# A low-rank mixer behind gated attention: down of the last batch's six chunks as two threes

## The chip, the cores and the metric

The kernel runs on one core of a Trainium2 chip. The core has a matrix engine (PE, with its weight loads shown apart as PEld), a vector engine (DVE), a scalar engine (ACT), a general engine (POOL) and a queue engine (SP) that only issues DMAs and handles semaphores. The engines run side by side and wait for one another by semaphores; each takes its own instructions strictly in order. The metric is the time of one execution on the device in microseconds (us).

## The reference

The inputs are `q`, `k`, `v`, `a_re`, `a_im` of shape (4, 8, 768, 48): four batches, eight heads, 768 steps, 48 numbers. The first half is a gated linear attention with a complex gate, the second a token mixer of low rank and a channel mixer. All is in float32.

```python
mag = sqrt(a_re**2 + a_im**2); scale = minimum(mag, 0.999) / (mag + 1e-6)
a_re_n, a_im_n = a_re * scale, a_im * scale
for t in range(S):                       # S_re, S_im: (B, H, 48, 48), zero at first
    new_re = ar * S_re - ai * S_im
    new_im = ar * S_im + ai * S_re
    S_re, S_im = new_re + outer(k[t], v[t]), new_im
    y[:, :, t] = q[t] @ S_re
x = y, heads side by side                # (4, 768, 384)
h = transpose(transpose(x) @ U @ V)      # U: (768, 32), V: (32, 768)
u = x + h
out = u + maximum(u @ w_ch1, 0) @ w_ch2  # w_ch1: (384, 1536), w_ch2: (1536, 384)
```

## The kernel before

**Tiling.** The 4 x 768 steps are cut in 24 chunks of 128 (`CH`). The attention takes one chunk after another: `prep(i)` (L847) weighs q and k, turns them on PE and keeps them in a tile `QK` of three in a ring; `chain(i)` (L881) computes the chunk's own products and the running state; the gates come from `gates(g)` (L649) for two chunks at a time. Each batch has six chunks, and its mixing starts when all six are there, since the product with U and V runs over all steps. `mixer(m)` (L974), m = 0 to 11, takes two chunks: `spread` and `mixed` make u in the tiles `xo` (one row of 384 for each step, L1016), `turned` transposes it to `uT`, then "up" is the product with `w_ch1` (`w1` in the code) and the maximum with 0, giving `h` (12 tiles of 128 channels by 256 steps), and "down" the product with `w_ch2` (`w2`), which is added to `xo`; `leave` stores the result. The last batch is m = 9, 10, 11, chunks 18 to 23.

**Fewer products.** From m = 2 on, up is done for two chunks at once as a product of a 3 by 3 by a 3 by 2 arrangement of blocks (`up_fewer`, L1110): 15 block products of 4 matmuls where the plain way has 18. Their right sides are sums of u's blocks (L1133), their left sides w1's blocks or sums of them, made once (L1214). They run as five chains A to E; in a chain PSUM accumulates, and after each step the chain's running total is added to one of the six outputs, so that a step's effect on the others cancels by the choice of the sums. From m = 1 on, down is done by `down_two` (L1253) as a 2 by 2 by 2 arrangement: 7 block products of 6 matmuls (128 by 128 times 128 by 192; `product` with its matmul in L1293) where the plain way has 8. For it the vector engine makes eight sums of h of 384 columns (L1285) and adds six totals of 192 and one of 384 to xo (`onto`, by L463). The sums of w2 that it needs stand in the tile `stage` (`W2S`), those of h in `stage` and `more` (`HS`).

**Order.** Every operation is added to a plan with an engine, a cost and what it reads and writes; but the sequence in which they are emitted is a list of numbers in the file, `ORDER` (L31), one common order for all engines. Each engine's instructions stand in that order. `Plan.order` (L151) checks that nothing comes before what it needs and that a ring's buffer is not taken too early. The costs do not decide anything when `ORDER` is there. DMA issues are in the same order: loads on SP, in-between moves and most stores on POOL; the stores of m = 11 on SP (L1237).

**The check at the end.** The quick form of the attention is valid only if the gates are in range. `judge` (L1418) reduces tables of minima and maxima, among them `least`, to one number: three pairs of small matmuls (L1433 to L1435, the group named "bad ps" in the plan) and a cast to `flag` (L1437). Behind the list of operations every engine loads that number into a register and branches on it:

```python
found = nc.values_load(flag, min_val=0, max_val=512, ...)   # L1468
with tc.If(found != 0, preferred_fallthrough_block=False):  # L1478
    in_general(...)                                          # the general, slow way
```

With the inputs at hand the number is 0, and the general way is not entered. L1523 carries the program's closing instructions.

## Time and profile before

The median of three executions is 536.64 us (536.31 to 537.48). The profiled execution took 537.17 us, with a span of 535.4 us from its first instruction to its last.

| | busy us | share of the span | instructions |
|---|---|---|---|
| PE (matmuls) | 515.6 | 96% | 7506 |
| PEld (weight loads) | 469.7 | 88% | 7506 |
| DVE | 419.7 | 78% | 837 |
| ACT | 295.3 | 55% | 528 |
| POOL | 32.2 | 6% | 61 |

DMA moved 39.95 MB, 75 GB/s on the mean; the granted clock of the matrix engine was 0.998 of full speed.

How to read the rows that follow in the prediction. A row of the 40 slices has one digit for each fortieth of the span, the busy share in tenths. A row of a group names line, engine, operation, result and sources, shapes (partitions by elements) and how often; behind the bar stand busy time, mean ns of one, and the idle time of the engine just ahead with what ended it. A row of the timeline starts with the start and the length in us. In the chain that ended last each row is a start, a length and the work that the end hung on. An engine's name with a q is its sequencer: loads of registers, branches, semaphores.

### The profile page before, as it was taken

The page shows a single profiled execution, that of the slowest core. Times are in us where ns is not written, and L with a number is a line of the kernel's source. Part 1 is how long each engine was busy: PE and PEld are TensorE (multiplying, and loading weights), DVE is VectorE, ACT ScalarE, POOL GpSimd, SP SyncE. Part 2 cuts the span into 40 slices and gives each one's busy share as a digit, 9 for nine tenths or more (in the row PEclk, how much of TensorE's full clock was granted, in tenths as well). Part 3 has the DMA queues.
Part 4 walks back from the last instruction along what each step waited for, and adds up shares of the span by engine and source line. Part 5 has one row for each costly group of instructions (what it writes and reads, how often), then busy time and mean ns, then how long its engine had stood idle before and what let it go on. Part 6 is the DMA issues. An engine that isn't in the chain of part 4 may idle for free.

```text
span 535.4 us, 17159 instructions
## 1 busy us (share of the span) xinstructions
PE 515.6 (96%) x7506; PEld 469.7 (88%) x7506; DVE 419.7 (78%) x837; ACT 295.3 (55%) x528; POOL 32.2 (6%) x61
## 2 busy tenths in 40 slices
PE   2899999999999999999999999999999999999995
PEld 1787786857989998999999999999999999999995
DVE  7898988999999997997887877797786735745543
ACT  5889998893776866546647847256345212020100
POOL 1000000001020001001100101100110000000010
PEclk9999999999999999999999999999999999999999
DMA  9967886565233424502524334200250000000011
GB/s 227 191 122 198 181 143 171 165 114 109 43 73 94 61 48 84 106 1 40 116 44 89 55 62 90 48 1 1 42 105 24 4 1 1 1 2 31 22 38 36
DMA packets 150690, 39.95 MB, mean 75 GB/s; under 512 B 145912, under 2 KB 147408, under 8 KB 150608
## 3 DMA queue, kind: packets, MB, share of 16 engines
q1 hardware_dynamic: 148400, 34.43, 32.3%
q0 software_dynamic: 2208, 4.35, 2.4%
q8 instruction: 61, 1.00, 0.8%
q14 instruction: 21, 0.17, 0.1%
HBM read 33.60 MB, written 4.76 MB: 72 GB/s over the span
## 4 chain that ended last, share of the span: by engine, by line
PE 82%; DVE 9%; ACT 4%; DMA 2%; issue 1%; SPq 1%; DVEq 0%; ACTq 0%
PE down L1293 29%; PE few L1161 13%; PE bank L1161 12%; PE bank L870 4%; PE bank L899 4%; PE bank L957 4%; PE bank L919 3%; PE bank L949 2%; PE up L1054 2%; PE bank L1016 1%; PE bank L745 1%; PE bank L809 1%; DVE QKC L460 1%; DMA stage<-in_moe_w_ch_dram 1%; ACT QK L876 1%
## 5 line engine op out<-in xcount | busy, mean ns | idle before, releaser
L1293 PE MATMUL down<-w,h 128*128 128x192 f32 x396 | 72.7, 330 | 0.0
L1293 PEld LDWEIGHTS down<-w,h 128*128 128x128 f32 x396 | 64.6, 190 | 1.0
L876 ACT COPY QK<-bank 112x512 f32<-112x512 f32 x96 | 51.3, 592 | 17.2 <-PE bank L870 17.0
L463 DVE TENSOR_TENSOR xo<-down,xo 128x192 f32<-128x192 f32 (+1 forms) x79 | 29.9, 385 | 30.9 <-PE down L1293 30.8
L457 ACT ACTIVATE gate<-gate 128x768 f32<-128x768 f32 (+1 forms) x50 | 39.7, 796 | 17.3 <-DVE wide L717 13.7
L460 DVE TENSOR_TENSOR QKC<-qk,cs 128x768 f32<-128x768 f32 x48 | 44.9, 952 | 3.7 <-ACT cs L457 3.6
L1169 ACT COPY h<-bank 128x512 f32<-128x512 f32 x25 | 14.6, 586 | 57.8 <-PE bank L1161 57.8
L1293 PE MATMUL down<-stage 128*128 128x192 f32 x198 | 37.9, 330 | 0.0
L1054 PE MATMUL up<-uT,w 128*128 128x256 f32 x144 | 34.0, 385 | 0.2
L1293 PEld LDWEIGHTS down<-stage 128*128 128x128 f32 x198 | 32.3, 190 | 0.8
L454 ACT ACT_TABLE_LOAD x24 | 30.8, 1283 | 1.1 <-PEq L1512 0.7
L1054 PEld LDWEIGHTS up<-uT,w 128*128 128x128 f32 x144 | 26.6, 190 | 5.0 <-DVE xo L463 0.5
L1237 POOL DMA_DIRECT2D out_dram<-xo x32 | 19.1, 625 | 193.6 <-DVE xo L463 104.8
L1169 ACT COPY h<-few 128x512 f32<-128x512 f32 x35 | 20.3, 586 | 18.5 <-PE few L1161 18.0
L870 PE MATMUL bank<-ident,QKC 64*112 64x64 f32 x768 | 29.1, 221 | 1.0 <-DVE G L466 0.4
L457 ACT ACTIVATE es<-bank 128x384 f32<-128x384 f32 x48 | 20.3, 495 | 17.6 <-PE bank L745 16.5
L1161 PE MATMUL bank<-extra,w 128*128 128x128 f32 x232 | 29.9, 275 | 0.0
L870 PEld LDWEIGHTS bank<-ident,QKC 64*112 64x112 f32 x768 | 24.3, 130 | 6.3 <-issue 1.6
L795 POOL DMA_DIRECT2D gate<-F x15 | 12.5, 834 | 284.8 <-DVE F L818 166.5
L969 ACT COPY xo<-bank 64x192 f32<-64x192 f32 x48 | 14.7, 314 | 24.6 <-PE bank L949 23.9
L1161 PEld LDWEIGHTS bank<-extra,w 128*128 128x128 f32 x232 | 28.1, 192 | 0.1
L457 ACT ACTIVATE cs<-F 128x384 f32<-128x384 f32 x48 | 23.7, 518 | 6.8 <-DVE F L818 6.6
(187 smaller groups left out, 1179.1 us busy)
## 6 DMA issues: line engine op xcount, KB each, us to landing
stage<-in_moe_w_ch_dram SPq DMA_DIRECT2D x12, 768.0 KB
gate<-in_a_re_dram SPq DMA_DIRECT2D x24, 192.0 KB
gate<-in_a_im_dram SPq DMA_DIRECT2D x24, 192.0 KB
qk<-in_q_dram SPq DMA_DIRECT2D x24, 192.0 KB
qk<-in_k_dram SPq DMA_DIRECT2D x24, 192.0 KB
VP<-in_v_dram SPq DMA_DIRECT2D x24, 192.0 KB
out_dram<-xo POOLq DMA_DIRECT2D x12, 192.0 KB, 2.4
out_dram<-xo POOLq DMA_DIRECT2D x20, 96.0 KB, 2.4
```

The source lines that it names most:

```text
L454: ACT(1.4, rank, lambda: nc.scalar.preload_act_table_set(name), writes=[TABLE])
L457: return nc.scalar.activation(out=o, in_=i, func=f, **kw)
L460: nc.vector.tensor_tensor(out=o, in0=a, in1=b, op=OP.mult)
L463: nc.vector.tensor_tensor(out=o, in0=a, in1=b, op=OP.add)
L870: nc.tensor.transpose(out=get(*ps[r])[0:DQ, h], in_=get(*qkc)[at, h].rearrange("p u d -> p (u d)")[:, 0:DQ], identity=ident[at, at], tile_ ...
L876: nc.scalar.copy(out=get(*QK)[:, u].rearrange("p (h t) -> p h t", t=CH)[:, :, r * HC:(r + 1) * HC], in_=get(*ps[r])[0:DQ])
L899: nc.tensor.matmul(out=get(*ps0)[r:r + HC, h], lhsT=k_of(h, r, HC), rhs=q_of(h, r, HC), start=True, stop=True, tile_position=(0, r))
L957: nc.tensor.matmul(out=get(*y[u])[side(r, u), p], lhsT=q_of(h, r * HC, HC), rhs=get(*(mid_G if r else ("G", i - 1)))[:, h], start=(p == 0) ...
L1054: nc.tensor.matmul(out=get(*ps)[:, e], lhsT=w1[:, f, (ff + e) * 128:(ff + e + 1) * 128], rhs=get(*uT)[:, f], start=(f == 0), stop=(f == KD ...
L1161: nc.tensor.matmul(out=get(*ps)[:, q], lhsT=w()[:, q * 128:(q + 1) * 128], rhs=v[0](), start=(n == 0 and q == 0), stop=True, skip_group_ch ...
L1169: ACT(c_act(n3 * CH) - 0.045, RU, lambda i=i, k=k: nc.scalar.copy(out=at(i, k), in_=get(*ps)), [ps], [o])
L1293: nc.tensor.matmul(out=get(*to)[:, part], lhsT=x(j), rhs=y[:, j], start=(first and j == 0), stop=(j == KH - 1), skip_group_check=not first)
```

## The change

- The constant `THREE` = 9. Mixers 1 to 8 keep `down_two`. Mixers 9, 10 and 11 no longer have a down of their own.
- In its place `down_three(t)`, t = 0 and 1, takes three chunks at once (18 to 20, 21 to 23) as a 3 by 3 by a 3 by 2 arrangement: three chunks, three thirds of the 1536 channels (4 tiles of 128), two halves of the 384 outputs. There are 15 block products of 4 matmuls of the same tile, in chains A to E as in `up_fewer`. For each t there are 13 sums of h's blocks of 512 columns and 15 additions of a total of 192 columns to `xo`.
- `prepare()`, called in mixer 9, makes w2's sums on the vector engine (3 of 384 columns, 12 of 768) and three copies of 384 columns on ACT. They stand in buffers that the attention has left (`qk`, `es`, `cs`, `QKC`, planes of the gate tile, `GL`) and one in `stage`.
- The h of mixers 10 and 11 stands in three buffers `hq` from the ring of `QK`, whose tiles get 128 partitions in place of `DQ` for it. The sums of h stand in `stage` for t = 0 and in `w1` for t = 1.
- Stores: chunks 18 to 20 go whole, on POOL; 21 and 23 whole and 22 in two halves, on SP.
- `ORDER` is changed. PE's order is the same up to its place 409 of 647, the end of mixer 5's down; behind that attention of chunks 18 to 23, mixers 6 to 8 and the last batch interleave anew: up of 9, 10 and 11, with the first three's products among the last of these, and then the second three. The six matmuls of `judge` are the last of PE and the cast to `flag` the last of DVE. Before that, on DVE, the copy of uT for mixer 1 stands behind two more steps, and the reductions into `least` of the groups 8 to 10 stand earlier, as does, on SP, the reload of the tables T that they read.

In the diff the lists of numbers in `ORDER` are left out but for the ones at the early and the last places.

```diff
@@ ORDER @@
...
-    608, 607, 605, 614, 726, 701, 64, 615, 441, 616, 251, 61, 442, 443, 444, 445, 255, 420, 56, 421, 256, 422, 423, 446, 60, 448, 59, 405, 447, 424,
-    406, 617, 618, 619, 620, 453, 494, 407, 57, 62, 704, 632, 257, 621, 63, 408, 495, 67, 496, 680, 634, 497, 414, 409, 70, 631, 454, 622, 635, 636,
+    608, 607, 605, 614, 726, 701, 64, 615, 441, 616, 251, 61, 442, 443, 444, 445, 255, 420, 56, 421, 256, 422, 423, 446, 60, 448, 59, 405, 424, 406,
+    617, 618, 447, 619, 620, 453, 494, 407, 57, 62, 704, 632, 257, 621, 63, 408, 495, 67, 496, 680, 634, 497, 414, 409, 70, 631, 454, 622, 635, 636,
...
-    2174, 2175, 2176, 2179, 2180, 2181, 2102, 2019, 2023, 2097,
+    2181, 2179, 2201, 2093, 2182, 2188, 2099, 2180, 2184, 2191, 1691, 2189, 2185, 2190, 2194, 2186, 2192, 2195, 2187, 2203, 2204, 2094, 2193, 2196,
+    2102,
@@ -344,6 +345,7 @@
     DH = DM // 2
     PLAIN = 1
+    THREE = 9
     FEWER, SINGLE, AHEAD = 2, 3, 1
     NCH = S // CH
     NT = B * NCH
@@ -848,7 +850,7 @@
-        buffer(QK, "QK", 3, [DQ, 2, H * CH])
+        buffer(QK, "QK", 3, [128, 2, H * CH])
...
@@ -998,12 +1000,30 @@
         uT, h = ("uT", m), ("h", m)
+        k3 = KF // 3
+        def third(n, j):
+            return ("h", n) if n == THREE else ("hq", ((n - THREE - 1) * 3 + j) // 2)
+        def third_of(n, j, k):
+            return third(n, j) + ((j, k),)
+        def third_at(n, j, k):
+            a = get(*third(n, j))
+            a = a[:, j * k3:(j + 1) * k3] if n == THREE else a[:, ((n - THREE - 1) * 3 + j) % 2].rearrange("p (f t) -> p f t", t=N)
+            return a[:, :, k * CH:(k + 1) * CH]
         if ahead or m >= AHEAD:
             buffer(uT, "uT", 2, [128, KD, N])
             if ahead:
                 ring(h, "hx", [extra.rearrange("p (f t) -> p f t", t=N)])
-            else:
+            elif m <= THREE:
                 buffer(h, "h", 1, [128, KF, N])
+            elif m == THREE + 1:
+                for n in range(KF // k3):
+                    buffer(("hq", n), "QK", 3, [128, 2, H * CH])
@@ -1148,7 +1168,7 @@
             put(1, lambda: x(11), lambda: b(2, 0), lambda: b(2, 1), OP.subtract, (), (11,))
             def at(i, k):
-                return get(*h)[:, n3 * i:n3 * (i + 1), k * CH:(k + 1) * CH]
+                return get(*h)[:, n3 * i:n3 * (i + 1), k * CH:(k + 1) * CH] if m < THREE else third_at(m, i, k)
             seen, left = set(), {}
             def chain(tag, steps):
@@ -1160,8 +1180,8 @@
                         for q in range(n3):
                             nc.tensor.matmul(out=get(*ps)[:, q], lhsT=w()[:, q * 128:(q + 1) * 128], rhs=v[0](), start=(n == 0 and q == 0),
                                              stop=True, skip_group_check=True)
-                    PE(0.893, RM, products, [uT, ("w1", 0, 0)] + [c_of(k) for k in range(8)] + [x_of(k) for k in v[1]], [ps], takes=[h],
-                       steps=2 * n3)
+                    PE(0.893, RM, products, [uT, ("w1", 0, 0)] + [c_of(k) for k in range(8)] + [x_of(k) for k in v[1]], [ps],
+                       takes=[h if m < THREE else third(m, to[0])], steps=2 * n3)
                     i, k = to
                     o = ("part", (m, i, k))
                     if to not in seen:
@@ -1172,7 +1192,7 @@
                     else:
                         DVE(c_dve(n3 * CH), RU, lambda i=i, k=k: nc.vector._custom_dve(
                             dve_ops.TENSOR_ADD_SAT, out=at(i, k), in0=get(*ps), in1=at(i, k), s0=math.inf, s1=0.0), [ps, o],
-                            [h + (n3 * i,), h + (n3 * i + 2,)])
+                            [h + (n3 * i,), h + (n3 * i + 2,)] if m < THREE else [third_of(m, i, k)])
                     left[to] = left.get(to, total_of[to]) - 1
                     yield
@@ -1332,6 +1352,161 @@
             product(two, 0, lambda j: of_s(2, j), w2_of(1, 1), lambda half: [("s2", 0, half)], first=False)
             onto(ua, 1, two, 0)
             leave(0, 1)
+        def w2_third(j, y, x=None):
+            a = w2[:, j * k3:(j + 1) * k3, y * DH:(y + 1) * DH]
+            return a if x is None else a.rearrange("p (j x) m -> p j x m", x=2)[:, :, x]
+        def w2_names(j):
+            return [("w2", f) for f in range(j * k3, (j + 1) * k3, 2)] + [("w2i", 0)]
+        def flat_of(n):
...
+        def second(j):
+            return lambda: flat_of(12 + j)
+        def prepare():
+            places = [("qk", None)] * 2 + [("es", None)] * 2 + [("cs", None)] * 2 + [("qkc", QKC)] * 3 + [
+                ("gx", AREA["x"]), ("gy", AREA["y"]), ("gar1", AREA["ar"][0:1])]
...
+            RW, W = ("w2x", 0), k3 * DH
+            for j in range(3):
+                DVE(c_dve(W // 2), RW, lambda j=j: nc.vector.tensor_tensor(
+                    out=flat_of(12 + j)[:, 0:k3:2], in0=w2_third(j, 1, 1), in1=w2_third(j, 1, 0), op=OP.subtract), w2_names(j), [("w2x", 12 + j, 0)])
+                ACT(c_act(W // 2), RW, lambda j=j: nc.scalar.copy(out=flat_of(12 + j)[:, 1:k3:2], in_=w2_third(j, 1, 1)), w2_names(j),
+                    [("w2x", 12 + j, 1)])
+            def b(j, k):
+                return (lambda: w2_third(j, 0), w2_names(j)) if k == 0 else (second(j), [("w2x", 12 + j)])
+            def x(n):
+                return (lambda: flat_of(n)), [("w2x", n)]
+            def put(n, p, q, op):
+                DVE(c_dve(W), RW, lambda: nc.vector.tensor_tensor(out=flat_of(n), in0=p[0](), in1=q[0](), op=op), p[1] + q[1],
+                    [("w2x", n)] + [("w2s", 0), ("s1", 0), ("s2", 0)] * (n == 11))
+            sub_, add_ = OP.subtract, OP.add
+            put(3, b(0, 0), b(1, 0), sub_)
+            put(4, x(3), b(2, 0), add_)
+            put(10, b(0, 0), b(2, 0), add_)
+            put(5, x(4), b(1, 1), add_)
+            put(8, b(0, 1), b(2, 1), add_)
+            put(6, b(2, 1), x(4), sub_)
+            put(1, b(0, 1), b(1, 1), sub_)
+            put(7, b(0, 0), b(2, 1), add_)
+            put(0, b(0, 0), b(1, 1), sub_)
+            put(2, b(1, 0), b(1, 1), sub_)
+            put(11, b(2, 0), b(2, 1), sub_)
+            put(9, b(0, 1), b(0, 0), sub_)
+        def down_three(t):
+            i1, RS = (B - 1) * NCH + 3 * t, ("three", t)
+            def a(i, j):
+                n, k = divmod(i1 + i, MC)
+                return (lambda: third_at(n, j, k)), [third_of(n, j, k)]
+            kept = [("hc", (t, n)) for n in range(8)]
+            def c_at(n):
+                if n in (0, 3):
+                    return a(0, 2)[0]() if n == 0 else a(2, 1)[0]()
+                z = {1: 0, 2: 1, 4: 2, 5: 3, 6: 4, 7: 5}[n]
+                place = w1[:, z // 3] if t else parts[z // 3]
+                return place[:, z % 3 * k3 * CH:(z % 3 + 1) * k3 * CH].rearrange("p (f t) -> p f t", t=CH)
+            def c_of3(n):
+                return a(0, 2)[1] if n == 0 else a(2, 1)[1] if n == 3 else [kept[n]]
+            def c(n):
+                return (lambda: c_at(n)), c_of3(n)
+            def put(n, p, q, op):
+                DVE(c_dve(k3 * CH), RS, lambda: nc.vector.tensor_tensor(out=c_at(n), in0=p[0](), in1=q[0](), op=op), p[1] + q[1],
+                    c_of3(n) + ([] if n in (0, 3) else [("w1", 0), ("w1", 1)] if t else [("w2s", 0), ("s1", 0), ("s2", 0)]))
+            sub_, add_ = OP.subtract, OP.add
+            put(6, a(2, 0), a(2, 1), add_)
+            put(4, c(6), a(0, 1), sub_)
+            put(5, c(6), a(1, 1), sub_)
+            put(6, a(1, 1), a(2, 1), sub_)
+            put(6, c(6), a(2, 2), sub_)
+            put(7, a(0, 2), a(0, 0), sub_)
+            put(2, a(1, 2), c(7), sub_)
+            put(1, c(7), a(2, 2), sub_)
+            put(7, a(0, 1), a(0, 2), add_)
+            put(7, c(7), a(1, 2), sub_)
+            put(3, a(1, 0), c(2), sub_)
+            put(3, c(3), c(5), sub_)
+            put(0, a(2, 2), a(0, 1), sub_)
+            def u(j, k):
+                return (lambda: w2_third(j, 0), w2_names(j)) if k == 0 else (second(j), [("w2x", 12 + j)])
+            def v(n):
+                return (lambda: flat_of(n)), [("w2x", n)]
+            total_of, seen = {(0, 0): 2, (0, 1): 3, (1, 0): 3, (1, 1): 2, (2, 0): 2, (2, 1): 3}, {}
+            def out_at(i, lo, hi):
+                n = i1 + i
+                b, cc = where(n)
+                def f(queue):
+                    queue.dma_start(out=out[b, cc * CH:(cc + 1) * CH, lo:hi], in_=get("xo", n)[:, lo:hi])
+                o = ("xo", n) if hi - lo == DM else ("xo", n, lo // DH)
+                if t:
+                    SP(0.6, ("load", 0), lambda: f(nc.sync), [o], [("out", n)])
+                else:
+                    POOL(0.55, R0, lambda: f(nc.gpsimd), [o], [("out", n)], late=0.6)
+            def run(tag, steps):
+                ps = ("down", (THREE + t, tag))
+                psum(ps, "Y", [128, DH], [128, 512])
+                for n, (w, x, to) in enumerate(steps):
+                    def products(n=n, w=w, x=x):
+                        for q in range(k3):
+                            nc.tensor.matmul(out=get(*ps), lhsT=w[0]()[:, q], rhs=x[0]()[:, q], start=(n == 0 and q == 0), stop=(q == k3 - 1),
+                                             skip_group_check=True)
+                    PE(1.3, ("mixing", THREE + t), products, w[1] + x[1], [ps], steps=2 * k3)
+                    i, k = to
+                    o = ("xo", i1 + i)
+                    def onto(o=o, k=k):
+                        z = get(*o)[:, k * DH:(k + 1) * DH]
+                        add(z, get(*ps), z)
+                    DVE(c_dve(DH), R0, onto, [ps], [o + (k,)])
+                    seen[to] = seen.get(to, 0) + 1
+                    if seen[to] == total_of[to]:
+                        if t and i == 1:
+                            out_at(i, k * DH, (k + 1) * DH)
+                        elif seen.get((i, 1 - k), 0) == total_of[(i, 1 - k)]:
+                            out_at(i, 0, DM)
+                    yield
+            A = run("A", [(c(0), v(4), (2, 0)), (a(2, 2), v(6), (2, 1)), (c(1), u(2, 1), (0, 1)), (c(2), v(7), (0, 0)),
+                          (c(3), u(0, 0), (1, 0)), (a(1, 0), v(9), (1, 1))])
+            Bc = run("B", [(a(0, 1), v(5), (0, 1)), (c(4), u(1, 1), (2, 1)), (c(5), v(0), (1, 1)), (a(1, 1), v(2), (1, 0)),
+                           (c(6), v(3), (2, 0))])
+            Cc = run("C", [(a(1, 2), v(11), (1, 0)), (c(7), v(10), (0, 0))])
+            D3 = run("D", [(a(0, 0), v(8), (0, 1))])
+            E = run("E", [(a(2, 0), v(1), (2, 1))])
+            for g in (A, Bc, D3, A, Bc, E, A, Bc, Cc, A, Bc, Cc, A, Bc, A):
+                next(g)
         if ahead:
             turned()
@@ -1361,7 +1536,12 @@
         if m == PLAIN:
             DVE(c_dve(KH * DH), R0, lambda: nc.vector.tensor_tensor(out=w2_of(0, 1), in0=w2_of(1, 1), in1=w2_of(0, 1),
                                                                     op=OP.subtract), [("w2s", 0)], ALL_W2 + [("w2i", 0)])
-        down_two()
+        if m < THREE:
+            down_two()
+        if m == THREE:
+            prepare()
+        elif m > THREE:
+            down_three(m - THREE - 1)
```

More of the change, by code (lines that the diff above doesn't have):

```diff
@@ new lines, in second @@
+        def second(j):
[3 more added lines that the diff above has]
+                ("gx", AREA["x"]), ("gy", AREA["y"]), ("gar1", AREA["ar"][0:1])]
+            shapes = {"qk": [128, 2, H, D], "es": [128, 2, DM], "cs": [128, H, 2, D]}
+            order = [12, 13, 3, 4, 10, 0, 1, 2, 5, 6, 7, 8, 14, 9]
+            for n, (tag, tiles) in zip(order, [("GL", GL), ("gai1", AREA["ai"][0:1])] + places):
+                if tiles is None:
+                    buffer(("w2x", n), tag, 2, shapes[tag])
+                else:
+                    ring(("w2x", n), tag, tiles)
+            RW, W = ("w2x", 0), k3 * DH
[24 more added lines that the diff above has]
+            put(9, b(0, 1), b(0, 0), sub_)
```

15 lines of the change are left out of this document (12 added, 3 removed), and 70 rows, old and new, of the table ORDER.

## The prediction

> **What bounds the kernel now.** I read the page first (totals and the 40 slices), then the busy time by stretches for the part that the change rewrites, then the timeline and the queue rows of the last microseconds, since those settle what follows the last matmul.
>
> ```profile
> span 535.4 us, 17159 instructions
> PE 515.6 (96%) x7506; PEld 469.7 (88%) x7506; DVE 419.7 (78%) x837; ACT 295.3 (55%) x528; POOL 32.2 (6%) x61
> PE   2899999999999999999999999999999999999995
> 516.32 13.67 PE down L1293 x84
> ```
>
> ```profile
> 330.00:430.00 100.00, 100.00 (x1691) 96.69 (x1690) 75.87 (x156) 45.52 (x90) 6.90 (x11) 1.00 0.17 35
> 430.00:460.00 30.00, 30.00 (x302) 28.70 (x301) 15.65 (x40) 4.80 (x10) 0.00 (x0) 1.00 0.01 2
> 460.00:490.00 30.00, 30.00 (x243) 29.46 (x242) 18.03 (x44) 4.00 (x7) 1.61 (x3) 1.00 0.04 14
> 490.00:515.00 25.00, 25.00 (x191) 24.71 (x190) 11.44 (x28) 3.52 (x6) 1.72 (x4) 1.00 0.04 13
> 515.00:536.00 21.00, 14.98 (x99) 14.61 (x98) 8.38 (x19) 0.00 (x0) 1.50 (x3) 0.93 0.14 46
> ```
>
> In a row of the second fence stand the bounds, the length, then the busy time of PE, PEld, DVE, ACT and POOL, the granted clock and the DMA share. PE is without a gap from 330 us to its last matmul at about 530 us, at clock 1.00, while DVE is half idle after 430 us. So from 330 us on the time is the number of matmuls times their pitch, plus what stands behind the last matmul. The whole kernel from 10% in is nearly so too; only the first slices are not.
>
> Behind the last matmul there are 5.4 us, and they need rows of their own:
>
> ```profile
> 514.94 0.19 PE L1433 MATMUL bank<-ones,bad 128*1 128x1 f32 x2
> 520.26 0.36 DVE L463 TENSOR_TENSOR xo<-down,xo 128x192 f32<-128x192 f32 x1 [1.21 <-PE down L1293]
> 520.53 0.14 DVE L1437 CAST flag<-bank 1x1 int32<-1x1 f32 x1
> ...
> 526.89 1.14 PE L1293 MATMUL down<-w,stage 128*128 128x192 f32 x6
> 527.86 1.14 PE L1293 MATMUL down<-w,h 128*128 128x192 f32 x6
> 528.84 1.14 PE L1293 MATMUL down<-w,more 128*128 128x192 f32 x6
> 529.04 0.56 DVE L463 TENSOR_TENSOR xo<-down,xo 128x384 f32<-128x384 f32 x1 [1.63 <-PE down L1293]
> 530.01 0.36 DVE L463 TENSOR_TENSOR xo<-down,xo 128x192 f32<-128x192 f32 x1 [0.42 <-PE down L1293]
> ```
>
> ```profile
> L1468 ACTq TENSOR_LOAD <-flag x1: 460/460/460, 520.7 to 520.7; - x1
> L1468 POOLq TENSOR_LOAD <-flag x1: 496/496/496, 520.7 to 520.7; - x1
> L1468 PEldq TENSOR_LOAD <-flag x1: 487/487/487, 527.5 to 527.5; - x1
> ```
>
> ```profile
> L1478 PEldq COMPARE_BRANCH  x2: 90/2116/4141, 528.1 to 530.3; - x2
> L1478 POOLq INC_SWDGE_SEM  x1: 1123/1123/1123, 521.8 to 521.8; - x1
> ```
>
> ```profile
> L1523 POOLq DRAIN  x3: 46/112/3975, 525.5 to 535.1; - x3
> L1523 SPq DRAIN  x3: 7/7/7, 534.2 to 534.8; - x3
> L1523 PEldq DRAIN  x2: 8/38/68, 534.5 to 534.9; - x2
> ```
>
> A queue row gives min/median/max in ns, then the first and the last start. The kernel sums up its range checks in one number (matmuls of L1433 to L1435, cast L1437); every engine loads it (L1468) and branches on it (L1478) to a fallback that is not entered. Today this is over early: cast at 520.53, POOL loads at 520.7, and its closing run (load, semaphore reset of 1.12, branches, a drain of 3.98 that starts at 525.5) ends at 529.4, hidden under the last ten microseconds of matmuls. It can only be the first of the three drains that took 3975 ns, as the others lie within the last 0.9 us. POOL then waits for PE, whose second branch (530.3, 4.14 long) and drain (534.5) are what the end at 535.4 hangs on.
>
> **Matmuls: fewer by six.** Mixers 9, 10, 11 did 7 products of 6 matmuls each, 3 x 42 = 126; the threes do 2 x 15 products of 4, 120. Matmul tile and stream stay 128x128 by 192. The PE rows above start 0.975 us apart for three matmuls (six records), 0.325 us each: 6 x 0.325 = **-1.95 us**, all on the bounding engine.
>
> **Vector work: about +20 us, on an engine that has room.** These rows price it:
>
> ```profile
> L460 DVE TENSOR_TENSOR QKC<-qk,cs 128x768 f32<-128x768 f32 x48 | 44.9, 952 | 3.7 <-ACT cs L457 3.6
> L463 DVE TENSOR_TENSOR xo<-down,xo 128x192 f32<-128x192 f32 x66 | 22.8, 353 | 28.3 <-PE down L1293 28.2
> L1285 DVE TENSOR_TENSOR h<-h 128x384 f32<-128x384 f32 x22 | 12.1, 551 | 0.0
> L463 DVE TENSOR_TENSOR xo<-down,xo 128x384 f32<-128x384 f32 x13 | 7.2, 552 | 2.6 <-PE down L1293 2.6
> L1214 DVE TENSOR_TENSOR extra<-extra,w 128x512 f32<-128x512 f32 x4 | 2.7, 684 | 0.0
> ```
>
> Added: w2's sums, 12 of 768 elements (12 x 0.952) and 3 of 384 (3 x 0.551); the sums of h, 26 of 512 (26 x 0.684); 30 adds of 192 (30 x 0.353): 11.4 + 1.7 + 17.8 + 10.6 = 41.5 us. Removed: 24 sums of 384 (13.2), 18 adds of 192 (6.4), 3 of 384 (1.7): 21.2. Net +20.3. From 430 us on DVE is idle for 106 - 53.5 = 52.5 us by the four stretch rows, and idle 24.1 of the 100 before that. ACT's three new copies of 384 lie in an engine that is busy under 5 us in 30. So I cost them at nothing as work; the cover is PE's unbroken run. What may cost is where they stand: a product of a three needs a whole sum first, and a total is added to xo before its PSUM tile's next step may run on, with five tiles in turn. Bounds: 0, since the order puts products of another mixer or another chain between two steps of one chain, and +2.0, about two waits as long as the 0.975 pitch of a product. Below nothing is excluded here, as PE has no gap from 330 us that could be filled. I take **+0.5**, near the lower end, since the old closing, with seven products through two tiles, shows no PE gap.
>
> **Moved in the common order.** Up to PE's place 409 of its order (some 329.5 us) no PE instruction moves. On DVE the copy of uT for mixer 1 moves behind two other steps:
>
> ```profile
> 90.02 0.56 DVE L1040 COPY uT<-bank 128x384 f32<-128x384 f32 x1 [0.89 <-PE bank L1035]
> ```
>
> It sat idle 0.89 us waiting here, and steps that were ready now go first. That gains up to 0.89 where DVE is the limit and nothing where PE is; the neighbouring slices of PE are full, so I take **-0.2** (bounds -0.9 and 0).
>
> The reductions 'least 8' to 'least 10' of the gate tables go earlier on DVE, the last from some 350 to about 330 us, and with it on SP's queue the reload of table T10 right behind the store of TD.
>
> ```profile
> 325.29 0.43 SPq L760 DMA_DIRECT2D TD<-es  x1
> SPq L763 <- DMA TD<-es: 4.9, 3, 2.2
> ```
>
> SP then waits for TD to land; the longest such wait was 2.2 us. Queued behind it are only input loads of chunks used much later. Store 325.3, landing 2.2 and the reload of the same order put T10 at about 330, when DVE comes to it; at most 1 us of DVE, which costs PE nothing at once. It is inside the +0.5 and its bounds. Outputs of chunks 18 to 20 go whole on POOL (48 issues become 45), the last three on SP (one more issue, of the kind of 0.4 to 0.6 us): 480 KB late in place of 288. They land while the engines close, so 0.
>
> **The closing: the check goes last.** In the changed order the matmuls of the check are the last instruction of PE and the cast is the last of DVE, behind the last add; before, both were some ten microseconds ahead. Nothing needs the number earlier; but every engine's load of it now waits for the end. Call T the end of the last product's matmuls. The last add now starts 0.03 after it (530.01 against 529.98), the cast 0.27 behind the add's start (520.53 against 520.26), the load 0.17 behind the cast: loads at T + 0.47. PE's own way from there is load 0.49, first branch 0.1 to 0.2, second branch 4.14, drain 0.07, some 0.3 between: T + 5.7. POOL's is its run of 520.7 to 529.4 (525.5 + 3.98), 8.7 us: **T + 9.2**. After the slowest engine comes the closing barrier, 0.9 us (PE's drain of 534.5 ends at 534.5, the span at 535.4). End at T + 10.1, where it was T + 5.4 (535.4 - 529.98): **+4.7 us** (4.66 unrounded). Bounds: by PE alone T + 6.6, +1.2 (POOL's drain free); above, +4.66 with 0.9 more if POOL's writes, which then end nearer, lengthen its drain.
>
> [...]
>
> **Sum.** -1.95 + 0.5 - 0.2 + 4.66 = +3.0. The profiled run of before took 537.17 (span 535.4 and 1.8 around it), 0.5 above the median 536.64 of the three; against the median: **539.6 us**, 0.56% slower. Its own range runs from 536.64 - 1.95 - 0.9 + 4.66 = 538.5 to 536.64 - 1.95 + 2.0 + 4.66 + 0.9 = 542.3. What a measurement tells from no change is about 0.2%, 1.07 us.
>
> **Rivals.**
> Rival 1: POOL's 3.98 us drain is not owed behind the check; it stood waiting for something that ends in any case (its last outputs, say), and would be short at the end. Then PE's branch sets the end, +1.2: -1.95 + 0.5 - 0.2 + 1.2 = -0.45, **536.2**. For it: the other two drains of POOL took 46 and 112 ns. Against it: the last of its outputs was issued by 516.5, 9 us before that drain, and such a write lands in 2.4 us (last figure of the second row).
>
> ```profile
> 514.36 2.14 POOL L1237 DMA_DIRECT2D out_dram<-xo  x4 [15.60 <-DVE xo L463]
> ```
>
> ```profile
> out_dram<-xo POOLq DMA_DIRECT2D x12, 192.0 KB, 2.4
> ```
>
>  [...]
>
> Rival 2, faster: the closing runs of both PE and POOL are waiting for something outside that starts at the last output, and the load's place costs nothing. Then -1.65: **535.0**. It decides if POOL needs less than 4.1 us from load to drain's end (T + 0.47 + 4.1 + 0.87 = T + 5.4) and PE too. Against it: POOL's run of before ended at 529.4, ahead of the last output.
>
> Rival 3: the new order stalls PE from 330 us on, by the 20 us of DVE or by T10; three or four waits of a product's pitch more than I took, +2 to +3.4: **541.6 to 543**. For it: the order puts the 30 products between other work, and whether their sums are ready there no row of before shows. Against: 52 us of idle DVE.
>
> **Chances.** My forecast 0.70, rival 1 0.13, rival 2 0.07, rival 3 0.10. The time is that of the first. The range 536.0 to 541.5 leaves out rival 2, rival 3 and the tip of the forecast's own, 0.2 in all. Faster by over 0.2%: rival 2 and 0.02 of rival 1 (its uT gain at the full 0.9); within 0.2%: the rest of rival 1; slower: forecast and rival 3.
>
> **What would show it.** The cast of the flag is the last DVE row, and all five loads of the flag start together at about 528.5 to 529. PE full from 330 us to a last matmul near 528.3, with 120 products' matmuls on the threes' line. POOL's semaphore reset, branch and a drain of about 4 us behind the loads, ending at 537 to 538 as the last before the closing barrier. If POOL's drain there is a fraction of a microsecond, rival 1 holds; if PE shows waits on DVE after 330 us that sum to over 2 us, rival 3. The prediction is wrong if PE's end comes later than 530, or the span's end less than 8 us behind it.

## The result, and the profile after

The changed kernel takes 541.01 us in the median (540.88 to 541.96, four executions) where the kernel before took 537.06 beside it: a ratio of 1.0078, 95% interval 1.0058 to 1.0097. It is slower, as forecast, by 3.95 us in place of 3.0. The profiled execution took 540.94 with a span of 539.1.

From the page of the changed kernel (span, totals, PE's row of the 40 slices), and its busy time by stretches (bounds, length, PE, PEld, DVE, ACT, POOL, clock, DMA share):

```profile
span 539.1 us, 17163 instructions
PE 514.8 (95%) x7494; PEld 468.9 (87%) x7494; DVE 438.3 (81%) x863; ACT 295.6 (55%) x531; POOL 30.5 (6%) x58
PE   2899999999999999999999999999999999999992
```

```profile
330.00:430.00 100.00, 99.92 (x1674) 96.59 (x1673) 78.27 (x150) 44.99 (x91) 6.85 (x11) 1.00 0.17 35
430.00:460.00 30.00, 30.00 (x301) 28.74 (x300) 18.72 (x48) 5.02 (x11) 1.08 (x2) 1.00 0.03 11
460.00:490.00 30.00, 30.00 (x268) 29.42 (x268) 24.72 (x52) 6.84 (x13) 0.00 (x0) 1.00 0.01 1
490.00:515.00 25.00, 25.00 (x164) 24.83 (x163) 19.50 (x42) 0.47 (x1) 1.07 (x2) 1.00 0.04 12
515.00:540.00 25.00, 14.00 (x91) 13.67 (x89) 5.42 (x18) 0.00 (x0) 1.07 (x2) 0.86 0.12 42
```

PE is nearly as full as before, and DVE is busier by the 19 us that were added; PE's last slice has a digit of 2 where it had 5. What changed most is the end. From the timeline of the changed kernel:

```profile
522.12 1.46 PE L1484 MATMUL bank<-stage,hq 128*128 128x192 f32 x8
523.42 1.46 PE L1484 MATMUL bank<-w,hq 128*128 128x192 f32 x8
...
527.32 1.46 PE L1484 MATMUL bank<-gate,hq 128*128 128x192 f32 x8
528.71 0.19 PE L1613 MATMUL bank<-ones,bad 128*1 128x1 f32 x2
...
528.82 0.36 DVE L465 TENSOR_TENSOR xo<-bank,xo 128x192 f32<-128x192 f32 x1 [0.68 <-PE bank L1484]
529.10 0.13 DVE L1617 CAST flag<-bank 1x1 int32<-1x1 f32 x1
```

And its queue rows behind that (min/median/max in ns, first and last start):

```profile
L1648 ACTq TENSOR_LOAD <-flag x1: 586/586/586, 529.3 to 529.3; - x1
L1648 POOLq TENSOR_LOAD <-flag x1: 612/612/612, 529.3 to 529.3; - x1
...
L1658 PEldq COMPARE_BRANCH  x2: 90/1946/3803, 530.0 to 530.3; - x2
L1658 POOLq INC_SWDGE_SEM  x1: 1063/1063/1063, 530.5 to 530.5; - x1
...
L1703 POOLq DRAIN  x3: 46/112/3728, 534.6 to 538.9; - x3
```

The last product ends at T = 527.32 + 1.46 = 528.78, 1.20 ahead of the kernel before (529.98). The loads of the flag start together at 529.3, T + 0.5 (SP's at 529.6). PE is through its long branch at 534.1. POOL's drain starts at 534.6 and ends at 538.28, and 0.86 us behind that the span ends: T + 10.36, where it was T + 5.39 (spans of 539.14 and 535.37, to two decimals). So the matmul part gained 1.20 us and the closing lost 4.97: +3.77 of span.

### The profile page after: what moved, and what is told of

It is laid out like the page before. It is cut to its first block, busy times and chain, and to the rows that moved or that the text cites. A ratio compares the mean times of both kernels' runs of the same rounds, so it can differ in the third digit from the quotient of the medians.

```text
span 539.1 us, 17163 instructions
## 1 busy us (share of the span) xinstructions
PE 514.8 (95%) x7494; PEld 468.9 (87%) x7494; DVE 438.3 (81%) x863; ACT 295.6 (55%) x531; POOL 30.5 (6%) x58
## 4 chain that ended last, share of the span: by engine, by line
PE 85%; DVE 9%; ACT 2%; issue 1%; DMA 1%; SPq 0%; DVEq 0%; ACTq 0%
PE down L1313 21%; PE few L1181 13%; PE bank L1181 12%; PE bank L1484 7%; PE bank L872 4%; PE bank L901 4%; PE bank L959 4%; PE up L1074 3%; PE bank L921 3%; PE bank L951 2%; PE bank L1036 1%; PE bank L747 1%; PE bank L811 1%; PE bank L751 1%; DVE QKC L462 1%
## 5 line engine op out<-in xcount | busy, mean ns | idle before, releaser
L878 ACT COPY QK<-bank 112x512 f32<-112x512 f32 x96 | 51.3, 591 | 20.3 <-PE bank L872 20.1
L1313 PE MATMUL down<-w,h 128*128 128x192 f32 x288 | 53.5, 331 | 0.0
L1313 PEld LDWEIGHTS down<-w,h 128*128 128x128 f32 x288 | 47.0, 190 | 0.8
L465 DVE TENSOR_TENSOR xo<-bank,xo 128x192 f32<-128x192 f32 x78 | 25.7, 351 | 16.7 <-PE bank L1484 12.2
L465 DVE TENSOR_TENSOR xo<-down,xo 128x192 f32<-128x192 f32 (+1 forms) x58 | 22.0, 387 | 11.8 <-PE down L1313 11.6
L459 ACT ACTIVATE es<-bank 128x384 f32<-128x384 f32 x48 | 20.3, 496 | 16.7 <-PE bank L747 15.6
L1313 PE MATMUL down<-stage 128*128 128x192 f32 x144 | 27.7, 331 | 0.0
L901 PE MATMUL bank<-QK 112*64 112x64 f32 x768 | 26.7, 224 | 0.0
L901 PEld LDWEIGHTS bank<-QK 112*64 112x64 f32 x768 | 24.2, 138 | 1.4 <-issue 0.2
```

Of the source, the lines that this page charges most:

```text
L459: return nc.scalar.activation(out=o, in_=i, func=f, **kw)
L465: nc.vector.tensor_tensor(out=o, in0=a, in1=b, op=OP.add)
L878: nc.scalar.copy(out=get(*QK)[0:DQ, u].rearrange("p (h t) -> p h t", t=CH)[:, :, r * HC:(r + 1) * HC], in_=get(*ps[r])[0:DQ])
L901: nc.tensor.matmul(out=get(*ps0)[r:r + HC, h], lhsT=k_of(h, r, HC), rhs=q_of(h, r, HC), start=True, stop=True, tile_position=(0, r))
L1313: nc.tensor.matmul(out=get(*to)[:, part], lhsT=x(j), rhs=y[:, j], start=(first and j == 0), stop=(j == KH - 1), skip_group_check=not first)
```

## The experiments

Times are compared with executions of the kernel before that were taken beside them. T is again the end of the last product.

**The check early again.** The check's steps are moved back ahead of the end (in this run the cast stands at 515.2, 14 us ahead of T); its PSUM tile comes from the ring that is free by then.

```diff
-        psum(ps, "T", [128, 1], [128, 512])      # in judge
+        psum(ps, "M", [128, 1], [128, 512])
 ORDER (numbers of the changed kernel):
-    2181, 2179, 2201, 2093, ... 2195, 2187, 2203, 2204, 2094, 2193, 2196, 2102,
+    2156, 2200, 2202, 2201, 2088, ... 2095, 2203, 2169, ... 2170, 2204, 2159, ... 2187, 2094, 2193, 2196, 2102,
```

> The changed kernel with one thing undone: the check's last steps (edges, three pairs of small matmuls, cast) stand some 17 us ahead of the end again; for this the check's PSUM tile is of the ring that the early mixers used. Theory (the check's place makes the tail): the last product's matmuls end at 528.8 as before, the span ends 5.4 us later at about 534.2, time about 536.0, 4.9 less than the changed kernel and 0.2% under the kernel before. Rival (the tail is made by the threes' later and larger outputs, 480 KB in place of 288): the span stays at 539.1, time 540.9. POOL's drain should again end ahead of PE's branch.

Measured: 536.32 us against 537.16, a ratio of 0.9988 (0.9979 to 0.9997); the span is 534.5. Its queue rows:

```profile
L1647 POOLq TENSOR_LOAD <-flag x1: 493/493/493, 521.5 to 521.5; - x1
L1647 PEldq TENSOR_LOAD <-flag x1: 492/492/492, 526.1 to 526.1; - x1
...
L1657 PEldq COMPARE_BRANCH  x2: 90/2055/4020, 526.7 to 529.4; - x2
...
L1702 POOLq DRAIN  x3: 46/112/3729, 528.0 to 534.2; - x3
```

POOL loads at 521.5 and its drain ends at 528.0 + 3.7 = 531.7, ahead of PE's branch (529.4 + 4.0). The threes and their late outputs are all still there, and 4.6 us of span are gone. The tail is owed to the check's place, and the rival that blames the outputs falls. One part of the expectation missed: T is 529.20 and not 528.8, since the check's six small matmuls stand ahead of T again.

**The check late in the kernel before.** One thing added to the old kernel:

```diff
 ORDER:
-    2179, 2180, 2181, 2102, 2019, 2023, 2097,
+    2179, 2188, 2180, 2189, 2181, 2102, 2019, 2023, 2097,
```

> The kernel before with one thing added: the check's small matmuls as the last of PE and its cast as the last of DVE. Theory: loads of the flag on all engines at 530.5, POOL's drain ends about 539, span about 540.1 (4.7 more), time 541.7. Rival (the tail needs the threes): span 535.4, time 537.

Measured: 542.53 against 537.16, 1.0103 (1.0088 to 1.0119), span 540.8.

```profile
L1468 POOLq TENSOR_LOAD <-flag x1: 646/646/646, 530.6 to 530.6; - x1
...
L1523 POOLq DRAIN  x3: 46/112/3974, 536.0 to 540.5; - x3
```

The same tail comes without any three: 5.4 us, 0.7 more than forecast, since POOL's run from load to the drain's end took 9.3 us (530.64 to 539.94) in place of 8.7, and T itself is 0.18 later in this execution.

**POOL's outputs on SP.** What is the drain's length owed to?

```diff
-                POOL(0.55, R0, lambda: f(nc.gpsimd), [o], [("out", i)], late=0.6)   # leave; the same in down_three
+                SP(0.6, ("load", 0), lambda: f(nc.sync), [o], [("out", i)])
```

> The changed kernel with all 29 outputs of POOL issued by SP, so that POOL issues 15 DMAs in place of 44. From before to after POOL's issues went from 47 to 44 and its drain from 3.98 to 3.73 us, both by 6%. Theory (the drain's length goes with the number of DMAs that POOL issued, 0.085 us each): drain about 1.3 us, semaphore reset shorter too; POOL is done at T + 6.3 and no longer the last by much, span 3 us shorter at about 536.0, time 537.9. Rival (a fixed drain of 3.7 us, or one that waits for something else): span 539.1, time 540.9. Loads behind the outputs on SP's queue may come later; if that stalls PE, T moves and is read apart.

Measured: 539.03 against 537.16, 1.0040 (1.0026 to 1.0054): about 2 us under the changed kernel, in place of 3.

```profile
L1658 PEldq COMPARE_BRANCH  x2: 90/2659/5228, 530.1 to 530.6; - x2
L1658 POOLq INC_SWDGE_SEM  x1: 478/478/478, 530.6 to 530.6; - x1
...
L1703 POOLq DRAIN  x3: 34/106/1369, 535.8 to 537.8; - x3
```

The drain is 1.37 us with 15 DMAs issued by POOL, 3.73 with 44 and 3.97 with 47: 0.081 us for each between 15 and 44, and 0.08 again between 44 and 47. The semaphore reset shrinks alike, 0.48, 1.06, 1.12. That part of the theory holds, and a fixed drain falls. The gain is smaller because the drain starts only at 535.8, 4.7 us behind POOL's last branch (the reset ends at 531.1; in the changed kernel it is 3.0), and PE's branch takes 5.23 us in place of 3.80. DVE's drain, too, starts 4.5 us behind its last branch, in the changed kernel 3.7. What makes these longer is not shown. In the trace's DMA records two 16 KB transfers of instructions behind the branches take 2.3 and 1.9 us (from 531.5 and 531.6), where the changed kernel has one of 1.3 (from 531.3); whether they have to do with it, no run tested.

**A hybrid order.** The threes behind the old order: up to the last batch's first up product the list of the kernel before, w2's sums put in as soon as their buffers are free; then the list of the changed kernel, with the check early.

```diff
 ORDER:
-    the changed kernel's list up to mixer 9's first up product
+    the list before up to there, with prepare's 11 first steps, and five others that the changed kernel had done by then, put between
```

> Check early as in the first run, and up to the first up product of the last batch the order of the kernel before (w2's sums put between); from there the changed kernel's order. From 329 us on the changed kernel shows 18 small waits of PE of 46 to 130 ns (1.1 us in all) where the kernel before has 5 (0.2 us); 13 of them lie ahead of the last batch's up. Theory (they come from the new order of the ups of mixers 6 to 8): 0.6 to 0.9 us off, last product ends at about 528.0, time about 535.2. Rival (they come from the vector engine's added work, or from elsewhere): time as in the first run, 536.0.

Measured: 539.74, 1.0052 (1.0039 to 1.0066): 3.4 us slower than the first run, not 0.9 faster. Rows of DVE and PE where PE waited, and the stretch of 430 to 460 us:

```profile
428.48 0.94 DVE L1403 TENSOR_TENSOR w2x<-w 128x768 f32<-128x768 f32 x1
430.11 0.68 PE L951 MATMUL bank<-VP,AT 64*64 64x48 f32 x32 [0.51 <-DVE AT L904]
...
446.23 0.36 DVE L465 TENSOR_TENSOR xo<-down,xo 128x192 f32<-128x192 f32 x1 [2.15 <-PE down L1313]
446.64 1.24 PE L1313 MATMUL down<-w,stage 128*128 128x192 f32 x6 [0.45 <-DVE xo L465]
448.91 2.94 PE L1181 MATMUL bank<-extra,w 128*128 128x128 f32 x24 [1.02 <-DVE extra L1153]
```

```profile
430.00:460.00 30.00, 28.41 (x303) 26.47 (x304) 16.60 (x42) 5.61 (x14) 1.08 (x2) 1.00 0.03 11
```

PE waits for DVE although DVE is busy for only 16.6 of 30 us. The waits are of two kinds. At 430.1 a sum of w2 (L1403) stands ahead of the copy to AT that PE needs, and PE waits 0.5 us; at 413.3 a smaller pause has the same cause. But the largest, at 448.9, and the one at 446.6 have no sum of w2 ahead of them: from 433 to 449 us DVE runs none, and it sits idle itself for 2.15 us, waiting for PE. They lie at the seam of the two lists. In the kernel before, the ups of mixer 9 stand between two products of the down:

```profile
443.84 2.84 PE L1161 MATMUL bank<-extra,w 128*128 128x128 f32 x24
448.31 1.14 PE L1293 MATMUL down<-w,stage 128*128 128x192 f32 x6
```

In the hybrid that product of the down comes first, waits for its PSUM tile to be added to xo, and DVE's sums of u for the ups come late behind it. By the starts of the matmuls these two pauses cost PE 1.85 of the 2.9 us that the hybrid loses against the first run from 325 us to T; those behind sums of w2, 0.9. So the run doesn't show that the old order has no place for w2's sums, and it says nothing on the small waits, which was its purpose.

**Early table reloads alone, in the kernel before.**

```diff
 ORDER:
-    1393, 1080, ... 1123, 1434, 1414, ... 1534, 1841, ... 1466, 1468,
+    1393, 1381, 1383, 1284, 1382, 1285, 1434, 1384, 1080, ... 1123, 1414, ... 1534, 1790, 1715, 1717, 1718, 1841, ... 1466, 1719, 1468,
```

(1434, a step of DVE on q and k, moves with them as in the changed kernel.)

> The kernel before with only the early moves of the table reloads: T8 to T10 and the reductions into least on DVE, the stores of TD and one load of a gate on SP stand where the changed kernel has them; uT's copy, the check and all products stay. In the changed kernel PE lacks a pause of some 0.4 us at 314.6 to 315.0 that three kernels with the order of before show (PE waits there for nothing that the profile names; its code block is fetched at 312.5 to 313.6, in the changed kernel at 311.5). Theory (the reload of T stood on SP ahead of input loads, waited 1.7 to 2.8 us for TD to land, and so put those loads on top of PE's fetch): SP's loads of 308 to 311 go out some 2 us sooner, the pause is gone, last product ends at about 529.5 in place of 529.98, time 536.6 against 537.1. Rival (the pause goes with other things): pause still there, time 537.1.

Measured: 536.03 against 536.82, 0.9986 (0.9976 to 0.9996). The rows at the pause; first the kernel before, PE and SP:

```profile
313.93 0.90 PE L949 MATMUL bank<-VP,AT 64*64 64x48 f32 x45
315.00 0.55 PE L949 MATMUL bank<-VP,AT 64*64 64x48 f32 x19 [0.17 <-issue]
315.48 1.24 PE L1293 MATMUL down<-stage,h 128*128 128x192 f32 x6
...
305.03 2.79 SPq L763 DMA_DIRECT2D T<-TD  x2
...
310.54 0.65 SPq L576 DMA_DIRECT2D VP<-in_v_dram  x1
```

then the changed kernel:

```profile
313.87 1.15 PE L951 MATMUL bank<-VP,AT 64*64 64x48 f32 x64
314.95 1.24 PE L1313 MATMUL down<-stage,h 128*128 128x192 f32 x6
...
308.41 0.83 SPq L578 DMA_DIRECT2D VP<-in_v_dram  x1
```

and this run:

```profile
314.07 1.15 PE L949 MATMUL bank<-VP,AT 64*64 64x48 f32 x64
315.15 0.76 PE L1293 MATMUL down<-stage,h 128*128 128x192 f32 x3
...
308.83 0.74 SPq L576 DMA_DIRECT2D VP<-in_v_dram  x1
```

Before, 64 matmuls are cut in 45 and 19, with a pause between; SP stood 2.8 us at the reload of T, and the loads behind it went out some 2 us later. With the reload moved, the loads are early and the pause is gone: the next product starts at 315.15 where it was 315.48, although this execution was 0.14 late just ahead. The moves together do it; the run doesn't part the reload of T from the stores of TD and the load of a gate that move with it. That the loads held up a fetch of PE's code, as the theory has it, is not shown: in the DMA records a 16 KB transfer of instructions ends at 313.6 in the kernel before, at 312.4 in the changed one and at 312.9 here, but no row ties the pause to it.

**w2's sums on POOL.**

```diff
-                DVE(c_dve(W), RW, lambda: nc.vector.tensor_tensor(out=flat_of(n), ...   # and the three of 384
+                POOL(c_dve(W), RW, lambda: nc.gpsimd.tensor_tensor(out=flat_of(n), ...
```

> The changed kernel with the check early again, and w2's 15 sums computed by POOL in place of DVE, at the same places of the order (396 to 450 us): 13 us of DVE's work taken away. Theory (DVE's added work is hidden and PE's small waits from 329 us on come from the order of the up products and their evacuations): small waits of PE stay at 1.1 to 1.2 us, last product's end within 0.3 of 529.2, time 536.0 to 536.6. Rival (DVE's load makes the small waits): up to 0.9 less, time 535.4. If POOL is slow with these sums or holds DVE up, the first threes' products wait, and time rises.

Measured: 546.29, 1.0181 (1.0160 to 1.0203). On the hybrid order the same edit:

> The hybrid order (order of before up to the last batch's up) with w2's sums on POOL. The hybrid's last product ended at 533.0, 3.8 us behind the first run's, with waits of PE on DVE of 0.3 to 1.2 us at 407, 413, 446 and 448 us. Theory (w2's sums stand in DVE's way there, since the order of before has no place for them): these waits go, last product at 529 or ahead of it, and if the order of before has the fewer small waits, at 528.2; time 535.2 to 536.5. Rival (the hybrid is late for another reason, a last product of mixer 8 or sums of u out of place): still 2 us or more over the first run.

Measured: 544.65, 1.0151 (1.0133 to 1.0170). Both are far over their theory's time and don't answer its question; that POOL may hold DVE up was foreseen for the first. In the second PE still waits 0.45 us at 445.7 ahead of the product that waited at 446.6 in the hybrid, with no sum of w2 on DVE. Two rows of the first one's timeline and one of its groups of DVE between 396 and 460 us:

```profile
409.94 1.81 POOL L1403 TENSOR_TENSOR gate<-GL,gate 128x768 f32<-128x768 f32 x1 [4.19 <-issue]
410.27 1.89 DVE L462 TENSOR_TENSOR G<-G,T 112x384 f32<-112x384 f32 x1
```

```profile
L465 DVE TENSOR_TENSOR xo<-bank,xo 128x192 f32<-128x192 f32 x8 | 2.7, 349 | 4.4 <-issue 4.4
```

POOL needs 1.8 us for a sum that takes DVE 0.95. And while it runs, a DVE step with two sources in SBUF can be held: 1.89 us for one of 112x384 that takes 0.55 in the changed kernel. Most such steps beside a sum of POOL were held, though not all: two of 128x768 kept their 0.95. The adds to xo with a source in PSUM were not held (349 ns here, 350 in the kernel before; 343 to 358 for those that run beside a sum of POOL).

**Half of w2's sums left out.** Nine of the sums are cut to 8 columns, in the kernel with the early check.

```diff
+                cut = (lambda a: a[:, 0:1, 0:8]) if n in (5, 6, 7, 8, 9, 11) else (lambda a: a)
-                DVE(c_dve(W), RW, lambda: nc.vector.tensor_tensor(out=flat_of(n), in0=p[0](), in1=q[0](), op=op), ...
+                DVE(c_dve(W), RW, lambda: nc.vector.tensor_tensor(out=cut(flat_of(n)), in0=cut(p[0]()), in1=cut(q[0]()), op=op), ...
```

> The changed kernel with the check early, and nine of w2's 15 sums cut to 8 columns (the three of 384 and sums 5 to 9 and 11 of 768; so the products that use them are wrong): about 7 us of DVE's work between 396 and 480 us is left out, nothing else is moved. Theory (the small waits of PE from 329 us on are evacuations behind each other in the new order of the ups, and DVE's added work is hidden): small waits of 46 to 130 ns still 1.0 to 1.2 us, last product within 0.2 of 529.2, time 536.3. Rival (DVE's load makes them): they fall by a half, last product 0.5 sooner, time 535.8.

Measured: 536.28 against 536.80, 0.9994 (0.9981 to 1.0007); the run with all sums had 536.32 against 537.16. By the starts of the matmuls both runs have 19 small waits of PE, 1.2 us in all, at the same places, and PE takes 204.2 us from the same product at 325 us to T in both. No gain: with the changed kernel's order these sums of w2 are hidden, as the theory has it.

**w2's sums later in the hybrid.** The same hybrid with the early table reloads; w2's sums stand behind the last batch's first up product, one after about three steps of DVE.

```diff
 ORDER:
-    prepare's steps between 396 and 450 us
+    prepare's steps spread between the vector steps of mixer 9's and 10's up
```

> Check early; up to the last batch's up the order of the kernel before, with the early table reloads that gained 0.14% there; w2's sums on DVE again, but spread behind the first up product of the last batch (one after every third step of DVE, about 445 to 480 us) in place of 396 to 450. Theory (the 1.3 us that the changed kernel gives back are the price of the new order of mixers 6 to 8, made to give w2's sums room): PE's waits on DVE at 407 to 448 us go, small waits ahead of 440 us are 0.3 us in place of 0.8, last product at about 528.2 to 528.6, time 535.4. Rival (w2's sums cost PE wherever they stand, since DVE then stands in the way of the evacuations of the up products): waits of PE on DVE between 445 and 490 us, last product at 529.5 or later, time 536.5 or more.

Measured: 540.54, 1.0072 (1.0059 to 1.0084). Two rows at its longest wait, then its stretch of 460 to 490 us (the first run has PE at 30.00 and DVE at 24.73 there) and one microsecond behind the wait:

```profile
459.94 0.95 DVE L1403 TENSOR_TENSOR w2x<-w 128x768 f32<-128x768 f32 x1
462.34 0.87 PE L1036 MATMUL bank<-r,V 32*128 32x96 f32 x14 [1.51 <-DVE h L1193]
```

```profile
460.00:490.00 30.00, 28.17 (x233) 26.84 (x233) 26.41 (x53) 6.15 (x11) 0.00 (x0) 0.94 0.00 1
```

```profile
464.00:465.00 1.00, 1.00 (x6) 1.00 (x6) 1.00 (x2) 0.00 (x0) 0.00 (x0) 0.50 0.00 0
```

The rival holds in part: with DVE at 26.4 of 30, PE is idle for 1.8 us between 460 and 490, 1.5 of them in one wait for an evacuation of h (L1193) that stands behind sums of w2. Behind that wait the granted clock is 0.50 from 463 to 466 us, which the busy times don't show; at half the pace some 1.5 us more are lost there (an estimate from the clock). A pause of 0.7 us at 443.9, at the seam, has again no sum of w2 ahead of it. Of the three places tried for w2's sums only the changed kernel's leaves PE full, but both others were tried with that seam.

## Why the prediction was right, and where its terms were off

| term | forecast, us | shown, us |
|---|---|---|
| six matmuls fewer | -1.95 | -1.95: products of four start 1.30 apart (522.12, 523.42), 0.325 each |
| the check's six small matmuls, now behind T | not in the sum | -0.39: from 325 us to T 203.79, with the check early 204.18 |
| tight places in the new order | +0.5 | +1.67: with the check early 0.28 is gained to T in place of 1.95 |
| early moves | -0.2 | -0.47: PE is 0.06 ahead at 313.9 and 0.53 at 315 |
| start of the two executions | 0 | -0.06 |
| closing | +4.66 | +4.97: T + 10.36 for T + 5.39 |
| sum, profiled executions | +3.0 | +3.77 (537.17 to 540.94) |

The second and third rows rest on one product that stands at the same place of PE's order in all kernels; the kernel before, the changed kernel and the run with the check early, and that run's last product:

```profile
325.52 1.24 PE L1293 MATMUL down<-w,h 128*128 128x192 f32 x6
324.99 1.24 PE L1313 MATMUL down<-w,h 128*128 128x192 f32 x6
325.02 1.24 PE L1313 MATMUL down<-w,h 128*128 128x192 f32 x6
527.74 1.46 PE L1484 MATMUL bank<-gate,hq 128*128 128x192 f32 x8
```

To T it is 204.46 us in the kernel before, 203.79 in the changed one and 204.18 with the check early (529.20 - 325.02).

The direction was right, and so was the mechanism that decides it, the closing. The time came out 1.4 us over the 539.6; 0.4 of that is the kernel before itself (537.06 beside the changed kernel, 536.64 in the forecast). That the sum of the terms is no further off than 0.8 us is in part luck: the tight places cost 1.2 us more than I took, and the check's matmuls and the reloads gave 0.7 back that the sum didn't have.

**Matmuls.** Right. In the threes' own part, from about 492 us to the last product, the starts of their matmuls stand 0.163 us apart in the median and nowhere more than 0.178. DVE's busy time rose by 18.6 us where I had summed 20.3; POOL's issues are 47 and 44 in the traces, where I wrote 48 and 45. Neither moves the sum.

**Tight places.** The step "I take +0.5, near the lower end" was mis-sized: 1.67, inside its bounds but near the upper one of 2.0. They are not where I looked for them. I argued about the threes' sums and totals, and these are hidden. In the single starts of the matmuls, 329 us to the end, PE shows 19 pauses of 46 to 130 ns (1.2 us), 17 of them in up products, that are no change of pattern (one that is shows in both kernels: 93 ns where a matmul with V follows a down product), where the kernel before has 5 (0.24 us); all of them lie ahead of 492 us, 12 ahead of the last batch's up. Beside them stand one of 0.29 us at 421.4, where a weight load waits for DVE, and 0.2 us at 460.7. The busy share doesn't show any of it: it stays at 99.9% and more up to 515 us. One of the larger ones, from the timeline of the changed kernel:

```profile
480.68 0.30 PEld L1181 LDWEIGHTS bank<-extra,w 128*128 128x128 f32 x2 [0.16 <-DVE extra L1153]
```

With nine of w2's sums cut they stay at their places and lengths, so those sums don't make them; that they come from the new order of the ups and their evacuations is what is left, and no run isolates it. The hybrids were meant to, and lost PE time at seams of their own. My phrase that the vector work costs "nothing as work" is shown for w2's sums in this order alone; the last hybrid, where one stood ahead of an evacuation, shows that the idle 52 us of DVE that I named as cover were no measure of it.

**Early moves.** The size was inside its bounds, the mechanism was wrong. I looked for the gain at uT's copy; PE is ahead by only 0.06 at 313.9, less than two executions of one order differ there (by 0.34 between the two runs with the check early). I took the table reloads for a cost of up to 1 us of DVE; `least` ran at 329.67 without a wait. The reloads and what moved with them on SP were worth 0.47 to PE, and 0.14% of the time (0.04 to 0.24) in a run of their own.

**Closing.** Right in place and in mechanism: loads at T + 0.5 (forecast 0.47), POOL's run 9.0 (8.7), barrier 0.9 (0.9). What the sum left out is that the check's matmuls, once behind T, no longer stand ahead of it. Rival 1, a drain not owed behind the check, falls: all 3.73 us of it ran after the check. Rival 2 falls too, since the span is 4.6 us shorter with the check early. Rival 3's waits on DVE beyond 2 us did not come.

**What the change is worth without the check's new place.** With the check early, the whole change is at 0.9988 of the kernel before; the early reloads alone are at 0.9986 with the old 126 matmuls. So of the six matmuls saved nothing is left that these times can tell from zero. In the profiles PE keeps 0.3 to 0.4 of their 1.95 us up to T (204.18 against 204.46, and 204.6 with the early reloads); the rest was paid out again in the new order. Both versions are faster than the kernel before and than the changed one. Whether some other order has room for w2's sums without the 1.67 us stays open; two were tried, and both had a seam that cost PE time of its own.

## What to carry to other kernels

Work that no result needs early may still have to end early: here a check whose value every engine loads starts the program's closing, and behind the last product that closing is bare (T + 10.36 for T + 5.39). Before an order is rewritten, look which engine's closing run is the longest, here POOL's 9 us, and keep what releases it that far ahead of the end. Price a vector step by the step that PE awaits behind it, not by the engine's idle share: a sum of 0.95 us on an engine that was busy for 16.6 of 30 us held PE for 0.5. And when an order is put together from two lists, look at the seam first: most of what the first hybrid lost was lost there, with none of the sums that it was built to test.

## What the runs showed of the hardware that I had not expected

- POOL's drain at the program's end went with the number of DMAs that it issued: 1.37 us for 15, 3.73 for 44, 3.97 for 47, about 0.08 us each; the semaphore reset ahead of it 0.48, 1.06 and 1.12.
- PE's branch over the fallback took between 3.36 us (half of w2's sums left out) and 4.14 (the kernel before) in ten of the eleven profiles, and 5.23 with POOL's outputs on SP. The ten spread over 0.78 us.
- While POOL ran a sum, a DVE step with two sources in SBUF took up to 1.89 us for 0.55; the adds to xo with a source in PSUM kept their 349 ns.
- With a table reload that takes 2.8 us on SP ahead of it, the load of VP was issued at 310.54 (308.83 with the reload moved); PE's pause ahead of 315.48 went when the reload and its neighbours on SP were moved, which in the changed kernel was worth 0.47 us to PE.
- After a wait of PE of 1.5 us the granted clock was 0.50 for 3 us (the last hybrid, 463 to 466), and 0.50 again after one of 4.0 us (the hybrid with w2's sums on POOL, 452 to 454); after one of 1.0 us it stayed at 1.00 (the first hybrid, 449 to 454).
